# Banded attention and mixture of experts: key blocks loaded once and mixed by copies on GpSimd

## The chip, the cores and the metric

The kernel runs on one core of a Trainium2 chip. A core has four engines that compute: TensorE (PE, with its weight loads listed apart as PEld), VectorE (DVE), ScalarE (ACT) and GpSimd (POOL); SyncE (SP) issues the DMAs. The metric is the device time of one execution in microseconds (us), over several runs of the same program.

## The reference

Inputs are q, k and v of shape (4, 8, 768, 64): batch, heads, sequence, head size. Attention is causal with a band of 96 keys, and the first 8 keys are seen by every row; the distance times a slope of the head is subtracted. Its output, as 3072 rows of 512, goes through a mixture of 8 experts whose gate is normalised by rows and columns in turn.

```
keep   = (pos_k < n_global) | ((rel >= 0) & (rel < n_local))      # 8, 96
dist   = where(is_global & ~is_local, n_local, abs(rel))
a      = softmax(where(keep, q @ k.T / sqrt(D) - slope[h] * dist, -1e9))
x      = (a @ v) as (3072, 512)
P      = exp(x @ w_gate), normalised 8 times by rows and by columns
out    = sum over e of  P[:, e] * (relu(x @ w1[e]) @ w2[e])
```

## The kernel before

**Tiles.** A block is 128 rows of the sequence, so a head has six. Work is done by head pairs: a pair n is (batch b, half, g), where half 0 ("early") is the first three blocks of queries and half 1 ("late") the last three, and g counts the four pairs of heads; there are 4 x 2 x 4 = 32 pairs. The two heads of a pair stand side by side in the 128 columns of a block, 64 each. A block of queries sees its own block of keys, the 96 keys before it, and the first 32 keys (of which 8 can count, by the inputs). The block of keys before it is therefore stored as a **mixed block**: its rows 0 to 31 are the first 32 keys of the head, its rows 32 to 127 those of the block before. Two key blocks then hold all that a block of queries sees, and only 1 for the very first block.

**Loading.** `load_qk` (L218) issues the DMAs of a pair's queries and keys on SP, `load_v` (L229) those of the values. Both use `load_pair` (L206) for what has mixed blocks. For an early pair that is one DMA per head for three plain blocks (L194) and two for the one mixed block 0 (L215, L216): slots 0 (mixed) and 1 to 3. For a late pair it is three DMAs per head (L196 to L198): plain blocks in slots 1, 3, 5, mixed ones in 0, 2, 4. Raw tiles of even pairs lie in a buffer that the later stage owns (named `acc` in the profile), those of odd pairs in tiles named `raw`; a raw tile is reused two pairs later.

**Preparing.** `prepare` (L241) takes a third of a pair at a time: part 0 turns the three query blocks on PE (L99, a transpose against the identity, into the PSUM tile `tp`), part 1 the first four key blocks, part 2 the last two of a late pair. Behind each, ACT rounds `tp` to the form that PE multiplies fastest (L259, `qh` or `kh`), and DVE subtracts to get the rest (L260, `ql` or `kl`). At the end of part 2 the loads of pair n + 2 are issued.

**Scores and values.** A score unit t is a third of a pair: one block of queries of both heads. `scores` (L264) multiplies three times for each (high by low, low by high, high by high) into two banks `s_ps`. `softmax` (L288) adds the bias and takes the minimum on DVE (L307), exponentiates on ACT (L311), and at the end of a pair adds a small constant and inverts on DVE (L314 and the line behind it). `turn` transposes the weights (`t_ps`), and `values` multiplies them by the values (`o_ps`). `flush` (L392) closes a pair: it issues the V loads of pair n + 2 and splits the output into `xh` and `xl`, the input of the experts.

**Order.** `unit` (L350) runs a batch in steps of two score units; 96 units make 48 steps. Scores run four units ahead of the values, `prepare` four more than that ahead of the values. A prologue in the first batch prepares pair 0, scales the first biases on DVE, scores two units, prepares pair 1, and then scales the biases of the other three pairs on POOL (`scale_bias`, L161, twelve instructions of line 168). PE keeps the order of the program. The other engines' order, and the place of the DMAs on SP, is set by a scheduler's own estimates; each engine then runs its queue strictly in order. A wait of one instruction holds all that stand behind it.

**Around it.** Between the steps the expert stage takes in what the attention has finished: `combine` (L639 to L653) forms sums and differences of `xh` and `xl`, nearly all on POOL, five operations a time, in bursts of twenty, and SP writes them out. POOL also rounds the gate (L549, L550) and the first weights (L571, L572), and sums weight blocks (L578). After the attention ends the experts' matrix products run to the end, on PE alone for most of the time.

Of the kernel before, what the change touches and what calls it, by code (L numbers as in the profile page):

```python
# [8 lines left out]
F32 = mybir.dt.float32  # L9
# [8 lines left out]
P = 128  # L18
# [83 lines left out]
class Banded:  # L102
# [1 line left out]


    SLOTS = 8 * len(GROUPS)
    RAW = UT * P + 4 * UT * P

    def __init__(self, tc, q, k, v, early):

        self.tc, self.nc = tc, tc.nc
        self.q, self.k, self.v = q, k, v
        self.H, self.D = q.shape[1], q.shape[3]
        H, nb = self.H, 3 * self.H * P
        self.bias1 = early[:, 0:2 * H * P].rearrange("p (h c) -> p h c", h=H)
        self.bias0 = early[:, 2 * H * P:nb].rearrange("p (h c) -> p h c", h=H)
        self.early_raw = early[:, nb:nb + self.RAW]
        nb += self.RAW
        self.d1 = early[:, nb:nb + 2 * P]
        self.d0 = early[:, nb + 2 * P:nb + 3 * P]  # L120
        self.work = [(b, half, g) for b in range(q.shape[0]) for half in range(2) for g in range(H // 2)]
        self.pending = []
        self.sums, self.inv, self.outs = {}, {}, {}
        self.pe = InOrder(tc)
        nb += 3 * P
        self.early_pT = early[:, nb:nb + 4 * P].rearrange("p (c k) -> p c k", c=4)
        assert nb + 4 * P <= early.shape[1] - 256
        self.warm = early[:, -256:].bitcast(mybir.dt.bfloat16)
        self.qk, self.vs, self.ready, self.scored = {}, {}, {}, {}

    def open(self, ctx, ident, idle):

# [49 lines left out]
    def raw_tile(self, n, first, width):  # L182


        if n % 2 == 0:
            t = self.early_raw[:, first * UT * P:(first + width) * UT * P]
        else:
            t = self.raw.tile([P, width * UT * P], F32, name=f"raw{width}")
        return t.rearrange("p (t c) -> p t c", c=P)

    def load_keys(self, dst, src, half, cols):
# [26 lines left out]
    def load_qk(self, n):  # L218
        if n >= len(self.work):
            return  # L220
        half = self.work[n][1]
        t = self.raw_tile(n, 0, 3)
        q_r, k_r = t[:, 0:UT], t[:, UT:]
        for src, cols in self.heads(self.q, n):
            self.nc.sync.dma_start(out=q_r[:, :, cols], in_=src[:, half * UT:(half + 1) * UT])
        self.load_pair(k_r, self.k, n)
        self.qk[n] = q_r, k_r

    def load_v(self, n):  # L229
        if n >= len(self.work):  # L230
            return
        self.vs[n] = self.raw_tile(n, 3, 2)
        self.load_pair(self.vs[n], self.v, n)

    def turned(self, name, part=None):
# [5 lines left out]
    def prepare(self, t):  # L241
# [3 lines left out]
        if n >= len(self.work):  # L245
            return
        nc = self.nc
        if part == 0:
            self.ready[n] = tuple(self.opd.tile([P, w * UT, P], F32R, name=name)
                                  for name, w in (("qh", 1), ("ql", 1), ("kh", 2), ("kl", 2)))  # L250
        q_r, k_r = self.qk[n]
        qh, ql, kh, kl = self.ready[n]
        nk = self.key_blocks(self.work[n][1])[0]
        src, hi, lo, n0, n1 = ((q_r, qh, ql, 0, UT), (k_r, kh, kl, 0, 4), (k_r, kh, kl, 4, nk))[part]
        if n1 > n0:
            tp = self.turned("tp", 3 * n + part)
            for t in range(n0, n1):
                self.pe.transpose(out=tp[:, t - n0], in_=src[:, t], identity=self.ident)
            nc.scalar.copy(out=hi[:, n0:n1], in_=tp[:, 0:n1 - n0])  # L259
            nc.vector.tensor_tensor(out=lo[:, n0:n1], in0=tp[:, 0:n1 - n0], in1=hi[:, n0:n1], op=ALU.subtract)  # L260
        if part == 2:
            self.load_qk(n + 2)

    def scores(self, ts):  # L264

# [4 lines left out]
        for c, t in enumerate(ts):  # L270
            n, group = divmod(t, len(GROUPS))
            blocks = self.key_blocks(self.work[n][1])[1]
            qh, ql, kh, kl = self.ready[n]
            s_list = []
            for j, i in GROUPS[group]:
                rows = slice(j * D, (j + 1) * D)
# [1068 lines left out]
```

## Time and profile before

| what | number |
|---|---|
| median of 3 runs | 2190.96 us (2190.64 to 2191.05) |
| the profiled execution's own time | 2187.54 us |
| its span in the profile | 2185.7 us |
| mean granted clock of PE | 0.991 |
| DMA, mean over the span | 209 GB/s |
| chain that ended last, share of PE | 87% |

The page of the profile lists each engine's busy time and share, the span in 40 slices, the DMA queues, the chain of work that ended last, and the costliest groups of instructions. A row of a group reads: line, engine, operation, tile written <- tiles read, shape, count | busy time, mean ns of one | idle time of the engine just ahead of them, with what ended it. Rows of the timeline begin with the start and the duration. All times are of one profiled execution.

```profile
PE   7998999999999999999999999999899999999998
PEld 5876777878888888888888888888678888888886
DVE  6665659755555555556777777777757777777777
ACT  6776753333332333324222222222142222222221
POOL 4453578667777777726777777777657777777774
PEclk9999999999999999999999999999999999999999
```

Each digit is a slice of 54.6 us. The attention fills the first five and a half: ACT is at its busiest there, and POOL at its least busy.

### The profile page before, as it was taken

The page shows a single profiled execution, that of the slowest core. Times are in us where ns is not written, and L with a number is a line of the kernel's source. Part 1 is how long each engine was busy: PE and PEld are TensorE (multiplying, and loading weights), DVE is VectorE, ACT ScalarE, POOL GpSimd, SP SyncE. Part 2 cuts the span into 40 slices and gives each one's busy share as a digit, 9 for nine tenths or more (in the row PEclk, how much of TensorE's full clock was granted, in tenths as well). Part 3 has the DMA queues.
Part 4 walks back from the last instruction along what each step waited for, and adds up shares of the span by engine and source line. Part 5 has one row for each costly group of instructions (what it writes and reads, how often), then busy time and mean ns, then how long its engine had stood idle before and what let it go on. Part 6 is the DMA issues. An engine that isn't in the chain of part 4 may idle for free.

```text
span 2185.7 us, 31313 instructions
## 1 busy us (share of the span) xinstructions
PE 2128.5 (97%) x10495; PEld 1745.4 (80%) x10495; DVE 1513.5 (69%) x2306; ACT 755.5 (35%) x1554; POOL 1472.7 (67%) x1236
## 2 busy tenths in 40 slices
PE   7998999999999999999999999999899999999998
PEld 5876777878888888888888888888678888888886
DVE  6665659755555555556777777777757777777777
ACT  6776753333332333324222222222142222222221
POOL 4453578667777777726777777777657777777774
PEclk9999999999999999999999999999999999999999
DMA  6676645666556656678776677767777776777772
GB/s 158 156 193 175 168 166 217 222 232 259 218 225 251 230 212 252 232 299 292 194 204 204 178 218 203 204 188 209 265 246 202 203 203 182 216 204 195 202 193 88
DMA packets 325322, 456.62 MB, mean 209 GB/s; under 512 B 132320, under 2 KB 187808, under 8 KB 314784
## 3 DMA queue, kind: packets, MB, share of 16 engines
q1 hardware_dynamic: 325152, 454.51, 66.9%
q8 instruction: 87, 1.43, 0.3%
q14 instruction: 83, 0.68, 0.1%
HBM read 315.12 MB, written 139.30 MB: 208 GB/s over the span
## 4 chain that ended last, share of the span: by engine, by line
PE 87%; DMA 3%; DVE 3%; POOL 3%; issue 1%; ACT 1%; SPq 1%; DVEq 0%; ACTq 0%; POOLq 0%
PE m_ps L96 26%; PE y_ps L96 15%; PE bank_z L96 11%; PE bank_w L96 11%; PE bank_x L96 11%; PE bank_y L96 5%; PE o_ps L96 2%; PE s_ps L96 2%; PE t_ps L99 1%; DMA w2f<-in_moe_w_dram 1%; PE h_ps L96 1%; PE tp L99 1%; POOL w1ops L562 1%; POOL wsum L578 1%; DMA w1f<-in_moe_w_dram 1%
## 5 line engine op out<-in xcount | busy, mean ns | idle before, releaser
L96 PE MATMUL m_ps<-hop,w2r 128*128 128x512 f32 x2520 | 639.5, 389 | 1.6 <-issue 1.5
L1251 DVE TENSOR_TENSOR m<-m_ps,m 128x1024 f32<-128x1024 f32 x406 | 495.6, 1221 | 194.4 <-PE m_ps L96 191.7
L96 PEld LDWEIGHTS m_ps<-hop,w2r 128*128 128x128 f32 x2520 | 472.8, 188 | 100.5 <-issue 2.4
L831 POOL TENSOR_TENSOR hop<-h,hop 128x512 fp32r<-128x512 f32 x180 | 234.1, 1301 | 310.4 <-ACT hop L830 305.4
L96 PE MATMUL y_ps<-w2ops,hop 128*128 128x512 f32 x1344 | 336.8, 389 | 0.0
L831 POOL TENSOR_TENSOR hop<-hsum,hop 128x512 fp32r<-128x512 f32 x240 | 306.2, 1299 | 1.7 <-ACT hop L830 1.7
L830 ACT CAST hop<-hsum 128x512 fp32r<-128x512 f32 x240 | 149.5, 623 | 432.1 <-POOL hsum L836 428.6
L96 PEld LDWEIGHTS y_ps<-w2ops,hop 128*128 128x128 f32 x1344 | 252.3, 188 | 52.5
L1101 DVE SCALAR_TENSOR_TENSOR acc<-y_ps,pm,acc 128x512 f32<-128x512 f32 x240 | 179.6, 750 | 139.0 <-PE y_ps L96 137.8
L830 ACT CAST hop<-h 128x512 fp32r<-128x512 f32 x180 | 111.8, 621 | 384.0 <-DVE h L842 373.0
L96 PE MATMUL bank_z<-xr,w1r 128*128 128x512 f32 x744 | 189.4, 390 | 0.0
L96 PE MATMUL bank_x<-xr,w1r 128*128 128x512 f32 x744 | 189.0, 389 | 0.1
L96 PE MATMUL bank_w<-xr,w1r 128*128 128x512 f32 x744 | 189.0, 389 | 0.0
L836 POOL TENSOR_TENSOR hsum<-h,h 128x512 f32<-128x512 f32 x120 | 153.4, 1300 | 48.8 <-DVE h L842 48.7
L96 PEld LDWEIGHTS bank_z<-xr,w1r 128*128 128x128 f32 x744 | 139.9, 188 | 29.0
L96 PEld LDWEIGHTS bank_x<-xr,w1r 128*128 128x128 f32 x744 | 139.5, 188 | 29.4 <-issue 0.5
L96 PEld LDWEIGHTS bank_w<-xr,w1r 128*128 128x128 f32 x744 | 139.5, 188 | 28.9
L836 POOL TENSOR_TENSOR hsum<-h,hsum 128x512 f32<-128x512 f32 x120 | 155.7, 1297 | 0.0
L578 POOL TENSOR_TENSOR wsum<-w1f 128x256 f32<-128x256 f32 x62 | 45.5, 754 | 101.8 <-DMA w1f<-in_moe_w_dram 101.8
L311 ACT ACTIVATE p_sb<-p_sb,mx 128x256 f32<-128x256 f32 (+1 forms) x192 | 92.5, 484 | 41.5 <-DVE mx L307 41.4
L96 PE MATMUL bank_y<-xr,w1r 128*128 128x512 f32 x372 | 94.4, 389 | 0.0
L707 DVE TENSOR_TENSOR t<-bank_y,t 128x512 f32<-128x512 f32 x93 | 64.2, 690 | 40.1 <-PE bank_y L96 36.9
(257 smaller groups left out, 3478.7 us busy)
## 6 DMA issues: line engine op xcount, KB each, us to landing
w1r<-w1s SPq DMA_DIRECT2D x434, 256.0 KB, 3.1
w2r<-w2s SPq DMA_DIRECT2D x420, 256.0 KB, 3.1
w1s<-w1ops SPq DMA_DIRECT2D x31, 1792.0 KB, 6.8
w2s<-s2ops SPq DMA_DIRECT2D x30, 1024.0 KB, 8.4
w2s<-w2ops SPq DMA_DIRECT2D x30, 768.0 KB, 7.6
w1f<-in_moe_w_dram SPq DMA_DIRECT2D x32, 512.0 KB, 7.8
w2f<-in_moe_w_dram SPq DMA_DIRECT2D x32, 512.0 KB, 8.6
xs_t<-piece SPq DMA_DIRECT2D x16, 512.0 KB, 3.4
```

What stands on the lines that cost most here:

```text
L96: return self.tc.keep_in_program_order(self.engine.matmul(*args, **kw))
L99: return self.tc.keep_in_program_order(self.engine.transpose(*args, **kw))
L311: nc.scalar.activation(out=pv, in_=pv, func=AF.Exp, bias=mx[:, u:u + 1], scale=-1.0, accum_out=sm[:, i, j:j + 1])
L562: self.nc.gpsimd.tensor_tensor(out=lo, in0=full, in1=hi, op=ALU.subtract)
L578: self.nc.gpsimd.tensor_tensor(out=s[:, n], in0=x, in1=y, op=op)
L707: tt(out=t, in0=bank["y"], in1=t, op=ALU.add)
L830: self.nc.scalar.copy(out=t[:, 0], in_=full)
L831: self.nc.gpsimd.tensor_tensor(out=t[:, 1], in0=full, in1=t[:, 0], op=ALU.subtract)
L836: self.nc.gpsimd.tensor_tensor(out=t, in0=self.full[x], in1=self.full[y], op=ALU.subtract)
L1101: nc.vector.scalar_tensor_tensor(out=a, in0=y_ps, scalar=moe.pm[:, tt, e:e + 1], in1=a, op0=ALU.mult, op1=ALU.add)
L1251: nc.vector.tensor_tensor(out=ms[p], in0=bank, in1=ms[p], op=ALU.add)
```

## The change

A pair's keys are now loaded as three plain blocks, like its queries, and turned once. The raw buffer of a pair shrinks from five to four times three blocks, and query and key tiles become one tile each for high and low parts, `qq` and `kk`; `kk` keeps its six slots. Part 0 of `prepare` turns the queries and part 1 the three key blocks, into slots 1 to 3 (early) or 1, 3, 5 (late); the loads of pair n + 2 are issued at the end of part 1. Part 2 fills the mixed slots with copies on POOL from the rounded halves. An early pair makes two mixed blocks, slot 0 of its own `kk` from the first 32 keys of slot 1 (L268) and 96 keys of slot 2 (L269), and the block `far`, which is kept for the late pair of the same heads, from slot 1 and slot 3. A late pair copies `far` into slot 0 (L272), the first 32 keys of `far` into slots 2 and 4 (L273), and the 96 keys of slots 1 and 3 into slots 2 and 4 (L274). Values are loaded as before.

```
-    RAW = UT * P + 4 * UT * P
+    RAW = 4 * UT * P
...
-        t = self.raw_tile(n, 0, 3)
+        t = self.raw_tile(n, 0, 2)
         q_r, k_r = t[:, 0:UT], t[:, UT:]
-        for src, cols in self.heads(self.q, n):
-            self.nc.sync.dma_start(out=q_r[:, :, cols], in_=src[:, half * UT:(half + 1) * UT])
-        self.load_pair(k_r, self.k, n)
+        for src, dst in ((self.q, q_r), (self.k, k_r)):
+            for rows, cols in self.heads(src, n):
+                self.nc.sync.dma_start(out=dst[:, :, cols], in_=rows[:, half * UT:(half + 1) * UT])
...
     def prepare(self, t):
...
+        G = MAX_GLOBAL
+        _, half, g = self.work[n]
         if part == 0:
-            self.ready[n] = tuple(self.opd.tile([P, w * UT, P], F32R, name=name)
-                                  for name, w in (("qh", 1), ("ql", 1), ("kh", 2), ("kl", 2)))
-        q_r, k_r = self.qk[n]
-        qh, ql, kh, kl = self.ready[n]
-        nk = self.key_blocks(self.work[n][1])[0]
-        src, hi, lo, n0, n1 = ((q_r, qh, ql, 0, UT), (k_r, kh, kl, 0, 4), (k_r, kh, kl, 4, nk))[part]
-        if n1 > n0:
-            tp = self.turned("tp", 3 * n + part)
-            for t in range(n0, n1):
-                self.pe.transpose(out=tp[:, t - n0], in_=src[:, t], identity=self.ident)
-            nc.scalar.copy(out=hi[:, n0:n1], in_=tp[:, 0:n1 - n0])
-            nc.vector.tensor_tensor(out=lo[:, n0:n1], in0=tp[:, 0:n1 - n0], in1=hi[:, n0:n1], op=ALU.subtract)
-        if part == 2:
-            self.load_qk(n + 2)
+            self.ready[n] = (self.opd.tile([P, 2, UT, P], F32R, name="qq"), self.opd.tile([P, 2, 2 * UT, P], F32R, name="kk"))
+        qq, kk = self.ready[n]
+        if part < 2:
+            src = self.qk[n][part]
+            dst = qq if part == 0 else kk[:, :, 1:1 + UT] if half == 0 else kk[:, :, 1::2]
+            tp = self.turned("tp", t)
+            for i in range(UT):
+                self.pe.transpose(out=tp[:, i], in_=src[:, i], identity=self.ident)
+            nc.scalar.copy(out=dst[:, 0], in_=tp[:, 0:UT])
+            nc.vector.tensor_tensor(out=dst[:, 1], in0=tp[:, 0:UT], in1=dst[:, 0], op=ALU.subtract)
+            if part == 1:
+                self.load_qk(n + 2)
+            return
+        copy = nc.gpsimd.tensor_copy
+        if half == 0:
+            self.far[g] = self.opd.tile([P, 2, P], F32R, name=f"far{g}", bufs=1)
+            for last, out in ((2, kk[:, :, 0]), (3, self.far[g])):
+                copy(out=out[:, :, 0:G], in_=kk[:, :, 1, 0:G])
+                copy(out=out[:, :, G:], in_=kk[:, :, last, G:])
+        else:
+            far = self.far[g]
+            copy(out=kk[:, :, 0], in_=far)
+            copy(out=kk[:, :, 2::2, 0:G], in_=far[:, :, 0:G].unsqueeze(2).broadcast_to([P, 2, UT - 1, G]))
+            copy(out=kk[:, :, 2::2, G:], in_=kk[:, :, 1:2 * UT - 2:2, G:])
```

The change also moves work in the queues. POOL's queue from its first operation that waits on another engine, before (line, operation, tile written <- tile read, shape; the rows of the biases, line 168, stand twelve times, the last one is shown):

```order
L168 TENSOR_SCALAR acc<-acc 128x256
L548 MEMSET ghl 128x512
L549 CAST ghl<-g_f 128x4x8
L550 TENSOR_TENSOR ghl<-g_f,ghl 128x4x8
L571 CAST w1h<-w1f 128x1024
L572 TENSOR_TENSOR w1l<-w1f,w1h 128x1024
```

The same place now, up to the first of the twelve biases (`far_324` and `far_392` are the blocks `far` of pairs 0 and 1; L583 is what L571 was):

```order
L268 COPY kk<-kk 128x2x32
L269 COPY kk<-kk 128x2x96
L268 COPY far_324<-kk 128x2x32
L269 COPY far_324<-kk 128x2x96
L561 CAST ghl<-g_f 128x4x8
L562 TENSOR_TENSOR ghl<-g_f,ghl 128x4x8
L583 CAST w1h<-w1f 128x1024
L268 COPY kk<-kk 128x2x32
L269 COPY kk<-kk 128x2x96
L268 COPY far_392<-kk 128x2x32
L269 COPY far_392<-kk 128x2x96
L168 TENSOR_SCALAR acc<-acc 128x128
```

The biases of pairs one to three moved behind the copies of pairs 0 and 1, the gate, and the rounding of the first weight, which reads `w1f` from a DMA.

SP's queue at the gate and the first weights, before (in this first batch pairs 4 and up are late; a row with x2 is two DMAs, one per head):

```order
L547 DMA g_f<-in_moe_w_gate_dram 128x4x8
L556 DMA w1f<-in_moe_w_dram 128x4x256
L225 DMA acc<-in_q_dram 128x3x64 x2
L196 DMA acc<-in_k_dram 128x3x64
L197 DMA acc<-in_k_dram 96x3x64
L198 DMA acc<-in_k_dram 32x3x64
L196 DMA acc<-in_k_dram 128x3x64
L197 DMA acc<-in_k_dram 96x3x64
L198 DMA acc<-in_k_dram 32x3x64
L557 DMA w2f<-in_moe_w_dram 128x2x512
```

And now:

```order
L559 DMA g_f<-in_moe_w_gate_dram 128x4x8
L568 DMA w1f<-in_moe_w_dram 128x4x256
L569 DMA w2f<-in_moe_w_dram 128x2x512
L226 DMA raw_387<-in_q_dram 128x3x64 x2
L226 DMA raw_387<-in_k_dram 128x3x64 x2
L226 DMA acc<-in_q_dram 128x3x64 x2
L226 DMA acc<-in_k_dram 128x3x64 x2
L226 DMA raw_563<-in_q_dram 128x3x64 x2
```

A pair's queries and keys are four issues, where those of a late pair were eight; the gate and the weights stand ahead of pair 3's loads now (`raw_387`), where they stood behind them. Ahead of `w1f` stand thirteen issues from pair 1's first load on: four each for queries and keys of pair 1, values of pair 1, queries and keys of pair 2, and the gate.

POOL's queue inside a burst of sums of x, before: five operations of one `combine`, in a row.

```order
L650 TENSOR_TENSOR xsum<-xh 128x512
L643 TENSOR_TENSOR xres<-xl 128x512
L651 TENSOR_TENSOR piece<-xsum,xres 128x512
L652 TENSOR_TENSOR xsum<-xsum,xres 128x512
L653 TENSOR_TENSOR piece<-xsum,piece 128x512
```

And now, in the late pairs of a batch (L655 and L662 to L665 are what L643 and L650 to L653 were):

```order
L665 TENSOR_TENSOR piece<-xsum,piece 128x512
L655 TENSOR_TENSOR xres<-piece,xl 128x512
L272 COPY kk<-far_1308 128x2x128
L273 COPY kk<-far_1308 128x2x2x32
L662 TENSOR_TENSOR xsum<-piece,xh 128x512
L663 TENSOR_TENSOR piece<-xsum,xres 128x512
L664 TENSOR_TENSOR xsum<-xsum,xres 128x512
L665 TENSOR_TENSOR piece<-xsum,piece 128x512
L274 COPY kk<-kk 128x2x2x96
L655 TENSOR_TENSOR xres<-xl,piece 128x512
```

The copies stand among the sums, and the sums behind L274 wait with it for the split of that pair's keys.

More of the change, by code (lines that the diff above doesn't have):

```diff
@@ L128, in __init__ @@
         self.warm = early[:, -256:].bitcast(mybir.dt.bfloat16)
-        self.qk, self.vs, self.ready, self.scored = {}, {}, {}, {}
+        self.qk, self.vs, self.ready, self.scored, self.far = {}, {}, {}, {}, {}
     def open(self, ctx, ident, idle):
@@ L187, in raw_tile @@
         else:
-            t = self.raw.tile([P, width * UT * P], F32, name=f"raw{width}")
+            t = self.raw.tile([P, width * UT * P], F32, name=f"raw{first}")
         return t.rearrange("p (t c) -> p t c", c=P)
@@ L231, in load_v @@
             return
-        self.vs[n] = self.raw_tile(n, 3, 2)
+        self.vs[n] = self.raw_tile(n, 2, 2)
         self.load_pair(self.vs[n], self.v, n)
@@ L272, in scores @@
             blocks = self.key_blocks(self.work[n][1])[1]
-            qh, ql, kh, kl = self.ready[n]
+            qh, ql, kh, kl = [o[:, i] for o in self.ready[n] for i in range(2)]
             s_list = []
```

## The prediction

> **What bounds the kernel now.** I read the page first, then the busy time of the engines in windows, then the waits of the attention stage, and last its timeline and groups. The page gives the span of the profiled execution, 2185.7 us, and one engine that is busy for nearly all of it:
>
> ```profile
> span 2185.7 us, 31313 instructions
> PE 2128.5 (97%) x10495; PEld 1745.4 (80%) x10495; DVE 1513.5 (69%) x2306; ACT 755.5 (35%) x1554; POOL 1472.7 (67%) x1236
> ```
>
> The change touches the attention alone. Its last values matmuls end near 309 us, so the windows are cut there (columns: stretch, its length, busy us of PE, PEld, DVE, ACT and POOL, then the granted clock, the DMA share and GB/s):
>
> ```profile
> 0.00:308.90 308.90, 280.13 (x2345) 221.00 (x2346) 194.31 (x687) 222.74 (x674) 152.90 (x140) 0.97 0.64 165
> 60.00:300.00 240.00, 223.46 (x1896) 178.88 (x1892) 152.86 (x528) 178.56 (x540) 129.37 (x101) 0.98 0.65 169
> 500.00:2185.00 1685.00, 1665.87 (x7351) 1376.27 (x7349) 1179.06 (x1392) 461.75 (x762) 1179.02 (x969) 1.00 0.69 215
> ```
>
> After 500 us PE idles 19 us in 1685: that part only moves earlier or later as a block. In the attention PE idles 28.8 us of 308.9, and from 60 to 300 us it is 93% busy, while ACT is 74%, DVE 64% and POOL 54% busy. So the attention is bound by PE's own work, with small stalls in between. What PE no longer does, or no longer waits for, comes off the time; what it newly waits for goes on. The waits of PE that concern this change, over the first 320 us (total, times, longest):
>
> ```profile
> PE s_ps L96 <- DVE kl L260: 7.3, 13, 2.5
> ...
> PE s_ps L96 <- DVE ql L260: 3.1, 8, 0.7
> PE o_ps L96 <- DMA acc<-in_v_dram: 2.9, 4, 1.5
> ...
> PE o_ps L96 <- DMA raw<-in_v_dram: 2.5, 2, 1.8
> ```
>
> Scores wait 10.4 us in 21 waits for the split of queries or keys, and the values matmuls wait 5.4 us for V loads that were issued late. No row has PE waiting for POOL.
>
> **The change part by part.** There are 32 head pairs, 16 in the early half of a batch and 16 in the late half.
>
> *Term A, transposes.* An early pair turns 3 key blocks and not 4, a late pair 3 and not 6: 16 x 1 + 16 x 3 = 64 fewer on PE. Their price, from the groups and three pieces of the timeline (start, us):
>
> ```profile
> L99 PE MATMUL tp<-ident,acc 128*128 128x128 f32 x128 | 22.5, 308 | 5.7 <-DVE m L148 2.9 <-DVE mx L307 1.8 <-DMA acc<-in_k_dram 0.9
> ...
> L99 PE MATMUL tp<-ident,raw 128*128 128x128 f32 x128 | 19.9, 278 | 0.5 <-DVE mx L307 0.5
> ```
>
> ```profile
> 36.87 0.44 PE L99 MATMUL tp<-ident,acc 128*128 128x128 f32 x2
> ...
> 40.08 0.87 PE L99 MATMUL tp<-ident,raw 128*128 128x128 f32 x6
> ...
> 46.18 0.98 PE L99 MATMUL tp<-ident,acc 128*128 128x128 f32 x7
> ```
>
> One more in a row costs 0.98 - 0.87 = 0.11 us; over all 256 PE's busy time per transpose is 42.4 / 256 = 0.166 us. So 64 of them are worth 7.0 to 10.6 us. Half of those that go stand in groups of two of their own, where one costs 0.22 us, so I take a value nearer the upper end: **-9 us**.
>
> *Term B1, loads.* All loads are issued by one queue, SP. Late pairs issue two key DMAs and not six, early pairs two and not four: 16 x 4 + 16 x 2 = 96 issues go. One occupies the queue for 0.43 to 0.48 us:
>
> ```profile
> 47.23 0.43 SPq L196 DMA_DIRECT2D raw<-in_k_dram  x1
> 47.71 0.48 SPq L197 DMA_DIRECT2D raw<-in_k_dram  x1
> 48.24 0.46 SPq L198 DMA_DIRECT2D raw<-in_k_dram  x1
> ```
>
> That is 96 x 0.46 = 44 us of SP time in 309. The V loads stand behind the key loads in this queue, and the 5.4 us of waits above are for V. A pair's query and key loads are also issued one step earlier now (behind the key transposes, not behind part 2); that puts four issues ahead of a V load, where up to eight stood. Bounds 0 and -5.4 us. Since a V load also waits for its buffer, I take half: **-2.7 us**.
>
> *Term B2, splitting the keys.* ACT rounds and DVE subtracts three blocks and not four, and the second pass of a late pair goes:
>
> ```profile
> L260 DVE TENSOR_TENSOR kl<-tp,kh 128x512 fp32r<-128x512 f32 x32 | 21.9, 684 | 5.6 <-ACT kh L259 5.6
> ...
> L259 ACT CAST kh<-tp 128x512 fp32r<-128x512 f32 x32 | 18.3, 573 | 0.7 <-PE tp L99 0.7
> ...
> L260 DVE TENSOR_TENSOR ql<-tp,qh 128x384 fp32r<-128x384 f32 x32 | 17.5, 546 | 1.8 <-ACT qh L259 1.8
> ...
> L259 ACT CAST qh<-tp 128x384 fp32r<-128x384 f32 x32 | 14.9, 467 | 8.5 <-PE tp L99 8.5
> ...
> L260 DVE TENSOR_TENSOR kl<-tp,kh 128x256 fp32r<-128x256 f32 x16 | 6.5, 409 | 1.8 <-ACT kh L259 1.7
> ```
>
> The three-block forms are those of the queries, so the chain to the rest of the keys is shorter by (573 - 467) + (684 - 546) = 244 ns, and each late pair is rid of a DVE pass of 409 ns and its ACT pass. The 13 waits for keys shrink by 13 x 0.244 = 3.2 us at least if they are this chain; none of it if they are DVE's queue; all 10.4 us if everything comes in time. I take **-3 us** (0 to -10.4).
>
> *Term C, the start of POOL.* POOL also makes the biases of pairs two to four (line 168, twelve operations). Before, they are the first thing it does, at 9.97 us. Now they stand behind the copies of the first two pairs, and the order shows more: into the wait for the second pair's keys came the rounding of a weight, which waits for its own DMA. All of POOL queues behind that. The rows (timeline, then groups):
>
> ```profile
> 8.83 0.92 SPq L225 DMA_DIRECT2D raw<-in_q_dram  x2
> 9.86 0.95 SPq L194 DMA_DIRECT2D raw<-in_k_dram  x2
> ...
> 9.97 8.52 POOL L168 TENSOR_SCALAR acc<-acc 128x128 f32<-128x128 f32 x12 [7.53 <-DVE acc L159]
> ...
> 19.08 0.28 DVE L307 CUSTOM_DVE_ANT_0 p_sb<-s_ps,acc 128x128 f32<-128x128 f32 x1
> ...
> 20.70 0.51 SPq L556 DMA_DIRECT2D w1f<-in_moe_w_dram  x1
> ...
> 21.20 0.28 PEld L96 LDWEIGHTS s_ps<-kl,qh 64*128 64x128 f32 x2 [0.33 <-DVE sm L315]
> ```
>
> ```profile
> 25.11 1.04 POOL L571 CAST w1h<-w1f 128x1024 fp32r<-128x1024 f32 x1 [0.85 <-DMA w1f<-in_moe_w_dram]
> ```
>
> ```profile
> L168 POOL TENSOR_SCALAR acc<-acc 128x256 f32<-128x256 f32 x6 | 5.2, 869 | 0.2
> ...
> L168 POOL TENSOR_SCALAR acc<-acc 128x128 f32<-128x128 f32 x6 | 3.2, 534 | 7.7 <-DVE acc L159 7.5
> ```
>
> SP resumes at 8.83 us and two issues take 1.03 us. Thirteen stand ahead of the weight now: 8.83 + 13 x 0.515 = 15.5. From issue to rounding took 25.11 - 20.70 = 4.4 us, so the rounding begins at 19.9 and ends at 21.0; four copies (1.2 us, below) bring 22.2. The second pair's first scores read the first and the third bias: 22.2 + 0.534 + 0.869 + 0.534 = 24.1 us, where DVE read the latter at 19.08. DVE runs in order and holds the score banks, so PE's next scores, at 21.20 before, come at about 24.5. That is 3.3 us late; the next pairs' biases are ready before they are read. Bounds: 0 if the idle time of the following 25 us swallows it, 5.0 us if the first delay carries through. I take the nearest row: **+3 us**.
>
> *Term D, the copies.* 16 x 4 + 16 x 3 = 112 copies on POOL. No such copy is in the trace; the nearest rows are two conversions, and above them the two-input form, with a small DVE row that shows how engines disturb each other (minimum, median, maximum ns):
>
> ```profile
> L571 POOL CAST w1h<-w1f 128x1024 fp32r<-128x1024 f32 x1 | 1.0, 1037 | 0.8 <-DMA w1f<-in_moe_w_dram 0.8
> ...
> L549 POOL CAST ghl<-g_f 128x32 fp32r<-128x32 f32 x1 | 0.2, 212 | 4.6 <-DMA g_f<-in_moe_w_gate_dram 4.6
> ```
>
> ```profile
> L578 POOL TENSOR_TENSOR wsum<-w2f 128x256 f32<-128x256 f32 x2 | 1.4, 738 | 0.0
> ```
>
> ```profile
> L314 DVE TENSOR_SCALAR sm<-sm x32: 163/174/1270, 20.5 to 296.7; 128x6 f32<-128x6 f32 x32
> ```
>
> ```profile
> L314 DVE TENSOR_SCALAR sm<-sm 128x6 f32<-128x6 f32 x32 | 16.3, 508 | 26.4 <-ACT p_sb L311 26.2
> ```
>
> ```profile
> 309.48 1.75 POOL L562 TENSOR_TENSOR w1ops<-w1f,w1ops 128x512 fp32r<-128x512 f32 x1 [9.42 <-ACT w1ops L561]
> ```
>
> The conversions give (1037 - 212) / 992 = 0.83 ns per element and 0.185 us beside. An early pair's four copies (64, 192, 64, 192 elements) are 1.17 us, a late pair's three (256, 128, 384) 1.19 us: 38 us in all. At 738 ns per 256 elements it would be 69 us. POOL is busy for 152.9 of 308.9 us, so there is room for either. What hides them: the transposes of a pair are issued a step or more ahead of the scores that use the mixed blocks, and a step is 308.9 / 48 = 6.4 us (96 score units, two to a step). The split takes 1 us, the copies 1.2, one of POOL's sums that stands ahead 1.3: 3.5 of 6.4. Queued behind a waiting copy on POOL are the sums of x, whose last, at 300 us, leave POOL idle for 9 us before it is needed again at 309.48. So the copies cost little: **+1 us**, between 0 and 3. The upper end is the L314 row: its mean is 508 ns in the same stretch (16.3 us in 32), 10.7 us over its median, and its long cases lie in POOL's sums; 38 us more of POOL on 153 would add 10.7 x 38 / 153 = 2.7 us to DVE.
>
> The Trainium skill, "SBUF — State Buffer", section "Who interferes with whom", says that GpSimd and a VectorE operation in a two-port mode hold a common pair of ports for a whole instruction, and the later one blocks. That speaks against giving copies to GpSimd. The maximum of 1270 ns, the length of one POOL sum, agrees; by that rule alone, with all of it on PE's path, the sum below would be -9.0 in place of -10.7.
>
> **Sum:** -9 - 2.7 - 3 + 3 + 1 = **-10.7 us**. The profiled execution took 2187.54 us (its span and 1.8 us around it); that gives 2176.8. It was 3.4 us below the median of the three timed runs, 2190.96, to which the forecast is put: **2180.3 us**.
>
> **The rivals.** *More comes free.* Some of the stalls pull the granted clock down:
>
> ```profile
> 120.00:140.00 20.00, 16.55 (x134) 13.43 (x132) 11.51 (x39) 13.21 (x42) 18.23 (x15) 0.95 0.76 197
> 140.00:160.00 20.00, 19.29 (x181) 15.51 (x181) 13.79 (x48) 15.85 (x49) 7.11 (x7) 0.97 0.69 183
> 160.00:180.00 20.00, 17.43 (x130) 13.68 (x130) 9.91 (x38) 12.66 (x40) 19.21 (x16) 0.83 0.76 200
> ```
>
> At these clocks PE's work there took 16.55 x 0.05 + 19.29 x 0.03 + 17.43 x 0.17 = 4.4 us longer. If the lighter SP queue ends the waits for V and half of those for keys, the sum is -9 - 5.4 - 6 - 4 + 3 + 1 = -20.4: **2170.6 us**. For it: SP is the queue that the V waits come from. Against: writes of x stand in that queue too, and now some of them wait for POOL's later sums. The Trainium skill, "TensorE: Matmul & The Clock Gate", section "HAM oscillation — how this bites in real kernels", has the clock fall when PE idles for a few microseconds; the 0.83 agrees.
>
> *Nothing comes free.* If the attention is held by the chain scores, maximum, exponential, transposes rather than by PE, the missing transposes become idle time. A and B1 give nothing, B2 its 3 us, C and D take 4: +1, some **2191 us**. For it: ACT is busy for 74% in stages that wait on each other. Against: PE's 93%.
>
> *Slower: POOL's queue becomes the last to finish.* POOL runs in order, and the last copy of a late pair (line 274) now stands between sums of x that themselves wait for data and for buffers. If in the 12 late pairs that fall into POOL's busy stretches the copies come one sum and one copy too late, each costs 1.3 + 0.5 = 1.8 us, 22 us together; with A at -9, B at -5.7, C and D at +4 that is +11: **2202 us**. It decides from the point where POOL is more than 6.4 - 3.5 = 2.9 us late against PE. For it: copies wait for a key split that is placed a step ahead only, and POOL was 96% busy in the window 160 to 180. Against: the order spreads sums and copies so that at most six or seven sums stand between two pairs' copies, about a step and a half, and early in a batch POOL has nothing else to do.
>
> **How the numbers follow.** Forecast 0.55, more free 0.20, nothing free 0.15, slower 0.10. The forecast with the nearer bounds of its terms spans 2174 to 2187; the range reaches to the fast rival and close to the null one: 2169 to 2191. A measurement of this kernel can tell about 0.2%, 4.4 us, from no change. Faster by more than that takes in the forecast and the fast rival, 0.75; the same 0.15; slower 0.10.
>
> **What would show it.** Right: 192 key and query transposes and not 256, with PE busy about 9 us less before the end of the attention; that end near 298 us; a first idle stretch of DVE between 19 and 24 us, ended by POOL's line 168; the V waits halved; PE waiting for POOL's copies under 2 us. Wrong: rows "s_ps <- POOL kk" of 10 us or more, copies above 1 us each, idle time of PE that has grown by the transposes' share, or an end of the attention that moves but a later stage that starts no earlier because POOL's sums end after it.

## The result, and the profile after

The changed kernel takes **2162.64 us** (median of 4 runs, 2162.28 to 2163.16), against 2190.80 us before (4 runs, 2188.39 to 2191.05). (In the later runs beside the experiments the kernel before had medians of 2188.46 to 2189.45 us, by which the gain is 26 to 27 us.) The ratio is 0.9877, with a 95% interval of 0.9865 to 0.9889. The forecast was 2180.3 us in a range of 2169 to 2191: the sign was right, the gain of 28 us is 2.6 times the 10.7 us of the sum, and it lies below the range.

The page of the changed kernel begins:

```profile
span 2160.2 us, 31171 instructions
PE 2114.1 (98%) x10431; PEld 1733.3 (80%) x10431; DVE 1504.2 (70%) x2290; ACT 746.7 (35%) x1538; POOL 1505.4 (70%) x1348
```

The span is 25.5 us shorter, PE has 64 instructions fewer and is 14.4 us less busy, and idles 46.1 us in place of 57.2. The windows of the stretch that the prediction looked at (columns as there):

```profile
60.00:300.00 240.00, 230.16 (x1944) 183.01 (x1943) 156.81 (x530) 180.43 (x543) 166.01 (x194) 1.00 0.63 170
...
120.00:140.00 20.00, 19.86 (x195) 16.36 (x193) 13.47 (x47) 16.43 (x51) 17.85 (x19) 1.00 0.83 224
140.00:160.00 20.00, 17.73 (x154) 13.53 (x153) 12.35 (x48) 14.54 (x48) 15.01 (x20) 1.00 0.76 194
160.00:180.00 20.00, 18.84 (x172) 14.44 (x170) 13.76 (x49) 15.66 (x51) 16.82 (x23) 1.00 0.79 211
```

The granted clock no longer falls to 0.95, 0.97 and 0.83 in these slices; it is full. And the waits of PE in the attention:

```profile
PE s_ps L96 <- DVE qq L260: 3.1, 9, 0.5
PE s_ps L96 <- DVE mx L319: 3.1, 2, 2.2
...
PE s_ps L96 <- DVE kk L260: 2.0, 4, 0.8
...
PE o_ps L96 <- DMA raw<-in_v_dram: 1.4, 1, 1.4
```

V waits fell from 5.4 to 1.4 us, waits for keys from 7.3 to 2.0 us. These 9 us are not 25.

Where the rest came from shows when the time is cut at the same work in both kernels. The multiplication on DVE that closes a pair (line 405 before, 417 after) is such a mark. These are the windows between the closings of pairs 4, 10, 24 and 31 (counted from 0), before, then after:

```profile
60.43:113.33 52.90, 51.04 (x455) 42.40 (x451) 36.29 (x126) 41.09 (x128) 25.42 (x20) 1.00 0.65 166
113.33:246.12 132.79, 119.20 (x1005) 93.29 (x1001) 80.86 (x287) 96.57 (x296) 60.44 (x48) 0.96 0.70 181
246.12:307.80 61.68, 60.58 (x498) 48.85 (x495) 37.39 (x118) 44.35 (x123) 43.58 (x34) 1.00 0.49 137
```

```profile
59.11:110.21 51.10, 49.81 (x445) 41.26 (x441) 34.41 (x125) 39.77 (x127) 25.05 (x37) 1.00 0.55 140
110.21:225.95 115.74, 109.57 (x979) 85.73 (x975) 77.97 (x281) 92.37 (x290) 79.03 (x99) 1.00 0.74 195
225.95:285.65 59.70, 59.15 (x486) 47.37 (x483) 34.77 (x114) 42.88 (x119) 50.06 (x51) 1.00 0.47 135
```

Of 25.5 us, 17.1 lie between pairs 10 and 24. There PE was only 90% busy before, at a clock of 0.96; ahead of it and behind it PE was 96% and 98% busy, and those two stretches gave 1.8 and 2.0 us. The start gave 1.3 us, and what follows the attention 3.35 us. So there were two bounds from pair 4 on: PE's work up to pair 10 and behind pair 24, and something else between them. The stretch between pairs 10 and 24 is called the middle below.

What it was stands in the queue of SP. Between the closings of pairs 10 and 24 it issued 221 DMAs before; their timeline rows add up to 119.0 of 132.8 us, and all its pauses over 0.2 us to 2.3 us. After, it issued 181; their rows add up to 99.9 of 115.7 us, and the pauses to 6.3 us. One piece of the timeline before shows how a full queue reaches PE without a V load:

```profile
129.90 0.87 SPq L977 DMA_DIRECT2D ys<-y_sb  x2
...
132.69 0.59 ACT L955 COPY y_sb<-y_ps 128x512 f32<-128x512 f32 x1 [3.31 <-DMA ys<-y_sb]
...
134.91 0.57 ACT L259 CAST kh<-tp 128x512 fp32r<-128x512 f32 x1
...
135.52 1.02 DVE L260 TENSOR_TENSOR kl<-tp,kh 128x512 fp32r<-128x512 f32 x2 [3.45 <-ACT kh L259]
...
136.35 0.68 PE L96 MATMUL s_ps<-kl,qh 64*128 64x256 f32 x2 [2.48 <-DVE kl L260]
```

SP gets to a write of expert results (`ys`) at 129.90 us, behind a row of loads without a pause. ACT waits 3.31 us for that write, because it fills the same buffer next; the rounding of keys stands behind it in ACT's queue, DVE waits for that, and PE for DVE. The table of PE's waits books these 2.48 us under "DVE kl".

### The profile page after: what moved, and what is told of

Same layout as the page of the kernel before. It is cut to its first block, busy times and chain, and to the rows that moved or that the text cites. A ratio compares the mean times of both kernels' runs of the same rounds, so it can differ in the third digit from the quotient of the medians.

```text
span 2160.2 us, 31171 instructions
## 1 busy us (share of the span) xinstructions
PE 2114.1 (98%) x10431; PEld 1733.3 (80%) x10431; DVE 1504.2 (70%) x2290; ACT 746.7 (35%) x1538; POOL 1505.4 (70%) x1348
## 4 chain that ended last, share of the span: by engine, by line
PE 87%; DMA 4%; POOL 3%; DVE 2%; ACT 1%; issue 1%; SPq 0%; POOLq 0%; DVEq 0%; ACTq 0%
PE m_ps L96 26%; PE y_ps L96 15%; PE bank_z L96 11%; PE bank_w L96 11%; PE bank_x L96 11%; PE bank_y L96 5%; PE s_ps L96 2%; PE o_ps L96 2%; PE t_ps L99 2%; DMA w2f<-in_moe_w_dram 1%; POOL wsum L590 1%; PE h_ps L96 1%; POOL w1ops L574 1%; DMA w1f<-in_moe_w_dram 1%; ACT p_sb L323 1%
```

## The experiments

All medians below are of the runs made beside the kernel before, whose median was 2188.46 to 2189.45 us then; the changed kernel was not run again with them, so a difference from it is one from its 2162.64 us above. At the end stands one table of the pieces of each profiled execution.

**Only the issues go.** The kernel before, with one DMA per head for the keys:

```
-        self.load_pair(k_r, self.k, n)
+        nk = self.key_blocks(half)[0]
+        for src, cols in self.heads(self.k, n):
+            self.nc.sync.dma_start(out=k_r[:, 0:nk, cols], in_=src[:, 0:nk])
```

> The kernel before, with the keys of a head brought in by one DMA that fills all four (early) or six (late) slots from consecutive blocks: 96 DMA issues fewer, the same bytes, the same transposes and splits. The mixed blocks hold other rows than they should. Theory 1 (the issuing queue, which was busy without a gap from 95 to 202 us, made the stalls of PE and the fall of its clock; the transposes are worth 64 x 0.163 = 10.4 us and no more): about 2171 us (2166 to 2176), V waits of PE under 1 us, granted clock 0.98 or more from 120 to 180 us. Theory 2 (the gain is PE's own work and what follows from it, the loads were hidden): 2188 us (2185 to 2191), clock still falling.

Measured: 2177.09 us, ratio 0.9948 (0.9933 to 0.9963), between the two forecasts, just outside the range of the first. The middle of the attention tells more than the sum (same columns):

```profile
115.10:234.01 118.91, 112.98 (x1005) 88.90 (x1001) 80.49 (x287) 95.50 (x296) 60.57 (x48) 1.00 0.79 200
```

The same 1005 matmuls took 132.79 us before and 118.91 now: 13.9 us less, of which 6.2 are busy time (119.20 to 112.98) and 7.7 idle time. The granted clock fell twice in the middle before, and does not fall here:

```profile
137.97:141.38 3.41, 3.41 (x22) 3.08 (x23) 2.75 (x11) 3.27 (x11) 3.17 (x4) 0.50 0.82 181
172.10:178.93 6.83, 6.09 (x41) 4.93 (x39) 2.81 (x12) 4.25 (x13) 6.59 (x6) 0.50 0.95 277
```

PE was busy for 9.50 us at half the clock, so the clock is about 4.8 of the 6.2 us (an estimate from these two rows). No wait for V is left in the middle. The other pieces moved by less than 1 us, but for a start that is 1.8 us longer. So the queue held the middle: 42 of the 96 issues lie in it, and without them it is 13.9 us shorter, where the whole term was 2.7.

**The issues come back.** The changed kernel, loading all key blocks as before, though only the plain ones are read:

```
-    RAW = 4 * UT * P
+    RAW = UT * P + 4 * UT * P
...
+        self.load_pair(k_r, self.k, n)
+        self.qk[n] = q_r, k_r[:, 1:1 + UT] if half == 0 else k_r[:, 1::2]
```

> The changed kernel, with all key blocks loaded as before (mixed ones too, which nothing reads): the 96 issues are back, transposes and copies stay as changed. Theory 1: 10 to 18 us back, 2173 to 2181 us, and the issuing queue again without gaps from about 95 us on. Theory 2: 2163 to 2166 us.

Measured: 2187.75 us, ratio 0.9995 (0.9985 to 1.0004): more than expected, the whole gain is gone. The middle and one slice of it, and then the V waits:

```profile
117.67:249.13 131.46, 115.44 (x979) 89.97 (x975) 78.77 (x281) 93.03 (x290) 78.92 (x99) 0.96 0.71 186
...
180.00:200.00 20.00, 14.29 (x100) 10.84 (x99) 8.74 (x29) 8.97 (x28) 8.33 (x11) 0.83 0.69 183
```

```profile
PE o_ps L96 <- DMA acc<-in_v_dram: 6.8, 4, 3.1
...
PE o_ps L96 <- DMA raw<-in_v_dram: 3.5, 5, 1.4
...
PE tp L99 <- DMA raw<-in_q_dram: 2.4, 1, 2.4
```

PE has 26 instructions fewer than before in the middle, and needs nearly as long: 131.46 against 132.79 us. Over the attention the waits for V are 10.3 us in place of 5.4. In the middle they are as before (5.6 and 5.4 us), but a wait of 2.4 us for a load of queries is new. PE is busy for 3.8 us less there and idles 2.4 us more, and the clock falls again. With the queue as the bound, less work on PE is worth little there.

**Issues without bytes.** The same again, with the added DMAs cut to one row each (`few=1` in `load_pair`, so that rows G to G + 1 and 0 to 1 are loaded).

> The changed kernel with the same number of DMA issues as the one with all key blocks loaded (2187.75 us), but the 96 additional ones bring one row of 64 numbers per block in place of 32 or 96 rows. Nothing reads them. If it is the number of issues in the one queue that costs: 2183 to 2189 us, queue without gaps from about 100 to 240 us. If it is the bytes and the contention of the DMA engines: 2162 to 2167 us. If it is the length of an issue that grows with its rows: between, 2168 to 2180 us, and issues shorter than 0.4 us.

Measured: 2194.57 us, ratio 1.0026 (1.0014 to 1.0037), slower than with full loads. 221 issues in the middle, busy 125.0 of 137.5 us. So it is not the bytes: without them nothing came back. The run does not hold the time of an issue equal, though: the issues of one row occupy the queue longer than the full ones (line 197, duration in ns as minimum, median and maximum; full loads, then one row):

```profile
L197 SPq DMA_DIRECT2D raw<-in_k_dram x16: 465/484/1025, 36.0 to 269.4; - x16
```

```profile
L197 SPq DMA_DIRECT2D raw<-in_k_dram x16: 662/672/721, 35.4 to 275.5; - x16
```

The middle is 6.0 us longer than with full loads, and the rows of the issues in it 5.7 us. So the time for which the issues hold the queue fits, and the bytes do not; why the small ones hold it longer was not pursued.

**Still fewer issues.** The changed kernel with values loaded by one DMA per head as well.

```
-        self.load_pair(self.vs[n], self.v, n)
+        nv = self.key_blocks(self.work[n][1])[0]
+        for rows, cols in self.heads(self.v, n):
+            self.nc.sync.dma_start(out=self.vs[n][:, 0:nv, cols], in_=rows[:, 0:nv])
```

> The changed kernel, with the values of a head brought in by one DMA that fills all four or six slots from consecutive blocks: 96 issues fewer again; the mixed blocks of values hold other rows than they should. If the queue still holds PE after the change (it has no gap from 110 to 150 and from 160 to 195 us, and PE idles 4.6 us between 120 and 200 us): 2154 to 2159 us. If the queue had become free enough: 2161 to 2164 us.

Measured: 2161.52 us, ratio 0.9876 (0.9860 to 0.9891), that is no change from the changed kernel. 137 issues leave 33 us of pauses in the middle, which takes 114.21 us in place of 115.74. So at about 180 issues the queue has all but stopped being the bound, though it pauses for only 6.3 us.

**The transposes come back.** The changed kernel with 64 transposes of the identity:

```
+            if part == 1:
+                self.pe.transpose(out=tp[:, UT], in_=self.ident, identity=self.ident)
...
+            tp = self.turned("tp", t)
+            for i in range(2):
+                self.pe.transpose(out=tp[:, i], in_=self.ident, identity=self.ident)
```

> The changed kernel with 64 transposes of the identity added, one in part 1 of every pair and two in part 2 of the late ones, which nothing reads. Theory 1: PE is bound by its work, so they cost what they last, 64 x 0.163 = 10.4 us: 2173 us (2170 to 2176), with the clock as after. Theory 2: 18 us or more, since stalls and the clock's falls come back with them: 2181 us. If they were hidden: 2163 us.

Measured: 2172.93 us, ratio 0.9930 (0.9916 to 0.9944), 10.3 us over the changed kernel, as theory 1 said, but only half for its reason. The middle:

```profile
112.47:230.41 117.94, 112.33 (x1005) 88.49 (x1001) 78.62 (x281) 92.49 (x289) 77.46 (x98) 1.00 0.73 191
```

26 more instructions are 2.76 us more of busy time, 0.106 us each, and the attention ends 5.2 us later (290.81 against 285.65). The other 4.6 us lie behind the attention; what they are made of is told in the last point of the next section.

**The second split comes back too**, by an ACT and a DVE pass over the last two of these blocks:

```
+            nc.scalar.copy(out=spare, in_=tp[:, 0:2])
+            nc.vector.tensor_tensor(out=spare, in0=tp[:, 0:2], in1=spare, op=ALU.subtract)
```

> As the one with the 64 transposes, and the last two of each late pair are also rounded on ACT and subtracted on DVE, into a tile that nothing reads. Theory 1: within 2 us of the one without the split (ACT and DVE have room): 2171 to 2177 us. Theory 3 (what went with the second pass on ACT and DVE is a good part of the gain): 5 us or more above it, 2178 us or more.

Measured: 2179.73 us, ratio 0.9958 (0.9944 to 0.9973), 6.8 us over the one before it, which looked like theory 3. The pieces speak against it: from pair 4 to pair 31 it is 0.4 us shorter than without the split. (The profiled execution is the fastest of its five, 4.3 us below their median; only 3.2 of the 6.8 us lie between the two profiled executions, 2175.39 and 2172.20 us.) The loss of 4.0 us lies ahead of the closing of pair 4, and 1.3 us of it ahead of that of pair 0 (33.06 against 31.79 us), when no late pair has been prepared, and only late pairs have the second pass. 3.0 of the 4.0 us are the granted clock: half of PE's busy time within its falls to 0.50 is 6.2 us in that piece, and 3.3 us without the split. Why it falls more there was not isolated.

**The copies, made twice**, on GpSimd:

```
-        copy = nc.gpsimd.tensor_copy
+        def copy(out, in_):
+            for _ in range(2):
+                nc.gpsimd.tensor_copy(out=out, in_=in_)
```

> The changed kernel with each of the 112 copies on GpSimd made twice: 38 us more of its time. Theory 1 (the copies are hidden, +1 us for the first set): 2162 to 2165 us. Rival (their delay or the shared access of GpSimd and VectorE reaches PE): 2167 us or more, with rows of PE waiting for the copies, or a mean of VectorE's small operations that rises.

Measured: 2202.27 us, ratio 1.0058 (1.0044 to 1.0071), far more than hidden. But 11.9 us of it are ahead of pair 4, 4.1 us in the middle, and 27 us behind the attention. So the copies were doubled again from the ninth pair on (`range(1 if n < 8 else 2)`):

> The changed kernel with the copies on GpSimd made twice from the ninth pair on, so that the start is as in the changed kernel: 28 us more of GpSimd. With all copies twice, 12 us were lost in the first four pairs, 4 us from there to the end of the attention, and 27 us behind it. Theory 1 (copies are hidden once the start is over): 2162 to 2166 us. Rival (GpSimd's backlog reaches the end of the attention, where VectorE, the gate's normalisation and PE wait for its last sums): 2180 us or more, with PE waiting for c_ps behind the attention.

Measured: 2190.57 us, ratio 1.0010 (1.0000 to 1.0020). The attention ends at 285.07 us, where it ended at 285.65: inside it, 28 us more of copies cost nothing. With the late start of the run before, the same doubled copies went with 4.1 us in the middle, so this holds for a start that is not late. Behind the attention they cost 23 us, 3.3 of them by the granted clock (in an execution 5.7 us below the median of its twelve). GpSimd's last sum of x (timeline), in the changed kernel and then here, with PE's longest wait here:

```profile
283.87 1.28 POOL L665 TENSOR_TENSOR xl<-xsum,xl 128x512 fp32r<-128x512 f32 x1
```

```profile
302.77 1.26 POOL L667 TENSOR_TENSOR xl<-xsum,xl 128x512 fp32r<-128x512 f32 x1
```

```profile
PE c_ps L810 <- DVE pm L807: 23.6, 4, 9.2
```

The changed kernel's sums end at 285.15, half a microsecond ahead of the attention; before, they ended at 300.06, 7.7 us ahead of it. The room is used up. Where the sums end 19 us later, the normalisation of the gate, which shares DVE with the last of x, and PE behind it wait.

**The copies on VectorE** (`copy = nc.vector.tensor_copy`):

> The changed kernel with the 112 copies on VectorE in place of GpSimd; GpSimd then starts with the biases as before the change. VectorE is 65% busy in the attention and gets about 25 us more. Theory 1 (what GpSimd gets is hidden behind the start, and only the start costs): the start is 3 us shorter, the rest the same: 2158 to 2162 us. Rival (VectorE stands in PE's chain, where each copy delays the next maximum): 2166 us or more. If the shared access of GpSimd and VectorE was a real cost of the change: below 2157 us.

Measured: 2183.64 us, ratio 0.9975 (0.9964 to 0.9985): 21 us worse than on GpSimd. The copies hold VectorE for 47.3 us, not 25, and the start is 3.7 us longer, not 3 us shorter. Pairs 4 to 10 take 58.08 us in place of 51.10, and PE's longest row of waits is for the maxima:

```profile
PE tp L99 <- DVE mx L319: 10.0, 5, 4.2
```

**The start.** The biases of the second pair of heads first (`scale_bias(1)` moved ahead of the first `prepare`):

> The changed kernel with the four biases of the second pair of heads put ahead of the copies in GpSimd's queue; the rest of that queue keeps its order at the start. Theory 1 (the late biases cost 3.1 us of PE's waits at 22 us): 2158.5 to 2161 us, first output of the attention closed at about 28.5 us in place of 31.6. Rival (the start's delay is swallowed later): 2162 to 2163.5 us.

Measured: 2170.12 us, ratio 0.9910 (0.9896 to 0.9924), 7.5 us worse. The first pair closed at 27.88 us in place of 31.64, as expected; but by pair 4 the kernel was 4.1 us behind. PE has a new row of waits in the start:

```profile
PE s_ps L96 <- POOL kk L269: 4.9, 2, 3.5
```

Copies of later pairs now stood behind the rounding of weights. The row is not the whole account: PE idles only 0.4 us longer in the start than in the changed kernel (13.9 against 13.5 us), and 3.0 of the 4.1 us are the granted clock (7.5 against 4.5 us by the same measure as above). With the row in view, the loads of those weights were then made to wait for the fourth pair's kept block, with the biases of one or two pairs first:

```
+            nc.gpsimd.tensor_copy(out=w1f[:, 0, 0:1], in_=after)
+            nc.gpsimd.tensor_copy(out=w2f[:, 0, 0:1], in_=after)
...
+                ws += [moe.plain_pair(0, f, stage, fw, attention.far[3][:, 0, 0:1] ...
```

> The changed kernel with the biases of the second pair of heads ahead of the copies in GpSimd's queue, and the loads of the first expert weights made to wait for the fourth pair's kept block, so that the rounding of weights stands behind the copies of the first four pairs. Theory 1 (the start is lost to GpSimd's queue: copies and biases behind the rounding, which waits for its DMA; putting only the biases first left PE waiting 4.9 us for copies): fourth pair closed at 45 to 47 us (49.2 in the changed kernel), median 2157 to 2160 us. Rival (the start is bound elsewhere, or what is won there is lost behind): 2161 to 2166 us.

> As the one before, with the biases of the second and third pair of heads ahead of the first copies. Theory 1: the same as it or up to 1 us better. Rival: the first copies then come late for the third score unit, 1 to 2 us worse than it.

Measured: 2160.76 us, ratio 0.9870 (0.9855 to 0.9885), with the biases of one pair first, and 2161.79 us, ratio 0.9879 (0.9862 to 0.9895), with those of two. They close the fourth pair at 48.30 and 46.60 us, where the changed kernel has 49.22, and pair 4, counted from 0, at 59.84 and 58.19 us, where it has 59.11. So what is won at the very start is mostly lost again by pair 4, as the rival of the first said. Neither reaches the gain of its theory 1, and neither can be told from the changed kernel or from the other; nothing that was run beats it by more than the runs scatter.

The pieces of each profiled execution, from the starts of the closing multiplications (us), and the issues in the middle piece:

| kernel | to pair 4 | 4 to 10 | 10 to 24 | 24 to 31 | behind | issues |
|---|---|---|---|---|---|---|
| before | 60.43 | 52.90 | 132.79 | 61.68 | 1877.9 | 221 |
| changed | 59.11 | 51.10 | 115.74 | 59.70 | 1874.6 | 181 |
| before, few issues | 62.20 | 52.90 | 118.91 | 61.75 | 1877.2 | 179 |
| changed, old loads | 63.72 | 53.95 | 131.46 | 60.31 | 1876.2 | 221 |
| changed, tiny loads | 64.43 | 52.30 | 137.46 | 63.89 | 1872.6 | 221 |
| changed, few V issues | 58.60 | 51.09 | 114.21 | 59.65 | 1877.0 | 137 |
| changed, transposes | 60.55 | 51.92 | 117.94 | 60.40 | 1879.2 | 181 |
| the same, with split | 64.53 | 51.91 | 117.31 | 60.66 | 1878.9 | |
| copies twice | 71.02 | 50.63 | 119.87 | 59.68 | 1901.4 | |
| copies twice, late | 58.60 | 50.62 | 116.15 | 59.70 | 1897.9 | |
| copies on VectorE | 62.80 | 58.08 | 120.45 | 63.64 | 1878.6 | 179 |
| one bias pair first | 63.25 | 51.07 | 115.52 | 59.64 | 1877.2 | |
| late weights, one | 59.84 | 51.08 | 116.00 | 59.63 | 1875.0 | |
| late weights, two | 58.19 | 51.05 | 116.06 | 59.65 | 1874.6 | |

Each row is one execution. Inside the attention a piece repeats well: changed, few V issues, one bias pair first and both with late weights agree within 0.1 us from pair 4 to 10 and from 24 to 31. The start and the piece behind repeat less well, since they hold falls of the granted clock to 0.50, each of about 3.4 us or a multiple of it but for the last, which the end cuts off. By half of PE's busy time within them, the clock costs 3.3 to 8.1 us in the start and 3.7 to 8.5 us behind the attention (without the kernels of doubled copies). A difference of 3 us there need not be the edit's.

## Why the prediction was wrong

**The step that failed** is the first: "So the attention is bound by PE's own work, with small stalls in between." PE's 93% was an average over three stretches of which two were bound by PE and the middle one by SP's queue. The windows list the engines that compute, and SP is none of them; the queue's own rows, 119 of 132.8 us busy in the middle, were not added up. None of the signs of being wrong that the prediction lists speaks of that queue, and none of them came; of its signs of being right, the waits for V fell by more than half and no row has PE waiting for copies, but the attention closes at 285.65 us, not near 298.

**B1, loads (-2.7, bounds 0 and -5.4).** The term's mechanism was right, its size was wrong: -13.9 us in the middle by the run with only the issues gone, and 15.7 us back by the one with the old loads. The bound of 5.4 us came from rows in which PE's last releaser is a V load. A late queue also reached PE through ACT's wait for a write (the chain above), and through the clock: about 4.8 of the 13.9 us. The rival "more comes free" had the lighter queue, the clock (4.4 us) and the waits for keys, but did not count SP's queue either. Its 6 us for "half of those for keys" are 5.2 by the prediction's own rows.

The Trainium skill, "TensorE: Matmul & The Clock Gate", section "HAM oscillation — how this bites in real kernels", would have idle stretches of PE over about 3.4 us pull the clock down. The runs agree that it falls with PE's stalls: with the issues gone the middle is at 1.00, with them added one slice is at 0.83 while PE is 71% busy in it. They do not agree on the length: before, the falls at 137.97 and 172.10 us came less than 2 us after idle stretches of 2.48 and 1.84 us, the longest of the middle.

**A, transposes (-9, bounds -7.0 and -10.6).** In place, 64 of them move the end of the attention by 5.2 us. One costs 0.106 us in the middle, the 0.11 of the lower price; the step "Half of those that go stand in groups of two of their own, where one costs 0.22 us, so I take a value nearer the upper end" was wrong, and part of them is hidden besides. The added ones wait for no load, as those that went did; that difference was not tested. And the price holds only where PE is the bound: with the old loads the missing transposes, split and copies together were worth 1.3 us of 132.8 in the middle.

**B2, the split (-3).** Right as far as the runs tell. The run with few issues and the one with transposes added have the same transposes on PE and nearly the same issues (179 and 181); they differ mainly in the width of the split, the copies and the place of the loads. From pair 4 to 31 the narrower one takes 230.26 us and the wider 233.56: 3.3 us, 2.0 of them idle time of PE. What the copies and the place of the loads do is in that sum too. The second pass of late pairs has no share in it.

**C, the start of POOL (+3).** The wait came where it was forecast:

```profile
21.77 8.35 POOL L168 TENSOR_SCALAR acc<-acc 128x128 f32<-128x128 f32 x12
...
22.33 0.29 DVE L319 CUSTOM_DVE_ANT_0 p_sb<-s_ps,acc 128x128 f32<-128x128 f32 x1 [0.32 <-POOL acc L168]
...
23.65 0.29 DVE L319 CUSTOM_DVE_ANT_0 p_sb<-s_ps,acc 128x128 f32<-128x128 f32 x1 [1.02 <-POOL acc L168]
...
22.68 0.38 PE L96 MATMUL s_ps<-kk,qq 64*128 64x256 f32 x1 [2.15 <-DVE mx L319]
...
24.00 1.21 PE L96 MATMUL s_ps<-kk,qq 64*128 64x256 f32 x11 [0.93 <-DVE mx L319]
```

The biases begin at 21.77 us (22.2 forecast), and PE waits 2.15 + 0.93 = 3.1 us (3.3 forecast). But the end hardly feels it: in the best start that was run PE idles 2.7 us less (10.9 against 13.5 us), and pair 4 closes only 0.9 us earlier. So the term is nearer to its bound of 0 than to the 3 us that were taken.

**D, the copies (+1).** Their time came out as forecast, 38.4 us in all; the rows agree with the price per element taken from the conversions (504, 397 and 238 ns by it). (The 69 us given there for the two-input row are a slip: at 738 ns per 256 elements, the 20480 elements of all copies make 59 us.)

```profile
L274 POOL CAST kk<-kk 128x384 fp32r<-128x384 f32 x16 | 8.1, 508 | 20.1 <-DVE kk L260 20.1
L272 POOL CAST kk<-far 128x256 fp32r<-128x256 f32 x16 | 6.5, 403 | 4.2 <-PE s_ps L96 4.2
...
L268 POOL CAST kk<-kk 128x64 fp32r<-128x64 f32 x16 | 3.9, 246 | 45.4 <-DVE kk L260 45.4
```

In the attention they cost nothing: doubled from the ninth pair on, they moved its end by -0.6 us. The rule of the Trainium skill that was weighed there, in "SBUF — State Buffer", section "Who interferes with whom", did not decide: the row of DVE's small operation after the change has a mean of 502 ns, and had 508 (its median rose from 174 to 392 ns). What was missed is the room behind them, 7.7 us before and 0.5 us now.

**Not in the sum:** 3.35 us behind the attention. PE idles 28.4 us there before and 24.5 us now; the clock goes the other way, 4.8 and 5.5 us by half of PE's busy time in its falls. The scheduler gave GpSimd there one order in the changed kernel, both with late weights, the one with few V issues and the one with copies on VectorE, and another in before, few issues, transposes, split, one bias pair first, old and tiny loads. PE's waits differ with it, before and then now:

```profile
PE y_ps L733 <- ACT hop L673: 2.6, 1, 2.6
...
PE y_ps L745 <- DVE fhop L674: 1.7, 1, 1.7
```

```profile
PE gt_ps L777 <- ACT g_sb L773: 1.3, 1, 1.3
...
PE y_ps L757 <- DVE fhop L686: 0.4, 1, 0.4
```

The first two stand in every kernel of the second order (2.1 to 2.7 and 1.7 to 1.8 us), the last two in every one of the first. That is 2.6 us of the 3.35. No run changed the order alone, so it is read from the waits and not tested. The 4.6 us that the transposes lost behind the attention are 2.2 us of idle time, that run being of the second order, and 3.0 us of clock, with two falls at 304.11 and 324.59 us that the changed kernel has not; its other work is 0.5 us shorter.

By steps from one kernel to the next, the 25.5 us of span are 12.7 for the issues (2185.7 to 2173.0), 3.0 for split, copies and the place of the loads (to 2170.0), and 9.8 for the transposes with the 4.6 behind the attention (to 2160.2). By the medians they are 11.4, 4.2 and 10.3. Taken in the other sequence, everything but the issues first, the first step gives 0.1 us (2185.6) and the issues the other 25.4.

## What to carry to other kernels

Cut the time at the same work in both kernels before averaging a busy share, and add up the DMA queue like an engine: a queue that hardly pauses can be the bound, even where few waits are booked to a DMA. Whether it is, a run with fewer issues and the same work tells: here 2.3 us of pauses in 133 were a bound, and 6.3 in 116 hardly one. Where two bounds stand close together, the price of an edit depends on which of them goes first; price each edit with the other bound taken away as well. Work moved to an engine with room is free only as long as the next hand-over from that engine keeps its margin, so look for when its last result is needed.

## What was not expected of the hardware

DMAs that bring one row held the queue longer than those that bring 96: 0.67 us against 0.48 us each (line 197, medians), and 125.0 against 119.3 us for 221 issues in the same stretch, of which only the added ones are small.

And the same copies of 64 elements had medians of 195 and 187 ns on VectorE, below the 238 ns of GpSimd, but means of 444 and 548 ns, where GpSimd had 246 and 242. Single ones lasted up to 1.28 us there, about as long as one of GpSimd's sums (1.27 to 1.31 us). That fits a wait for GpSimd, but no run isolates it.
